# Attention beside a long convolution: U interleaved by VectorE instead of GpSimd, last taps on SP's queue, other durations in the plan

## The chip, the core and the metric

The kernel runs on one core of a Trainium2 chip. The core has TensorE (PE in the profile, its weight loads PEld), ScalarE (ACT), VectorE (DVE), GpSimd (POOL) and SyncE (SP), each with a list of instructions of its own that it takes in order, and 16 DMA engines. The metric is the device time of one execution in microseconds (us).

## What is computed

Two branches over a sequence of 2048 rows of 448 features, mixed by a gate per row:

```python
g = sigmoid((x * gate_w).sum(-1, keepdims=True))
q, k, v = (x @ wq) in 16 heads of 28, x @ wk, x @ wv          # one key and value head for all
a = concat(softmax(q k^T / sqrt(28)) v) @ wo
K = einsum("dn,dnl,dn->dl", C, exp(dt*A*l), dt*B).real          # 256 complex modes, l = 0..2047
b = causal_convolution(x, K) + x * Dskip                        # per feature; by FFT in the reference
out = g * a + (1 - g) * b
```

The reference calls the second branch with the same x: u is x, and the input B_u is not read.

## The kernel before, in words

**Attention.** For each of 4 query blocks of 512 rows and 4 groups of 4 heads (16 steps i), 64 tiles of scores (16 key tiles by 4 heads, 128 x 512 each) are made on TensorE (L1289, or L1312 with the masked copy qM of the queries), turned into exponentials on ScalarE (L1344, in turns over three and two tiles at once, 410 instructions in all, written to a ring of 15 tiles) and multiplied with the values on TensorE (L1362). Five PSUM banks hold the scores, so the matmuls of one turn fill the banks that the turn before has left. VectorE copies each step's result away (L1127) and divides it (L1139); the output projection of a block (`outp`, L1109) is folded into O on VectorE (`fold`, L1118). `qproj` (L857, L863, L866, L869) makes the next step's queries, and GpSimd's queue issues the DMAs that spread them into qM.

**Convolution.** The 448 features are taken in 14 blocks c of 32. `masters` (L896 to L916) squares the modes' factors, `tables` (L936 to L986) builds tables of powers on VectorE, five levels of products (L950) and sums (L965) of doubling size, then L973, L979 and L986. `kgen` (L1009) makes 32 features' taps from a table on TensorE in two halves; VectorE copies each to kstg (L1019), and four DMAs per half write it to a scratch tensor KP in DRAM. `tload` reads KP back as shifted rows (T or, late, U's space) on SP's queue. `conv` (L1071) multiplies the taps with U, VectorE scales the product (L1080), L1091 transposes it, and VectorE adds it to O (L1100). Each block has two convolutions, 28 in all.

**U.** U is x with its rows interleaved, so that a matmul can read it as weights. SP's queue loads it into O as 16 strips in two groups of eight (("ust", 0) and ("ust", 1), in `loads`). `prep_u` then copies it, half of the features into U and half into a part of T, with two strips to an instruction: 16 GpSimd copies (L598) of 128 x 448 bf16. Six shifted copies U<-U per group of blocks follow on SP's queue once all of the first half's are done; the other half is moved to U later by `ufill`. O is set to zero when all 16 copies are done.

**The order of the work** is not written by hand. Each operation is entered with an engine, a duration in ns, what it reads and writes, and a priority `pr` (lower first). `Prog.schedule` runs a greedy simulation: among all operations it takes the one that could start earliest, then by `pr`, and so fixes every engine's list. Durations come from `el(n, rate, fix) = fix + n / rate`, with 68 ns and 0.96 elements per ns by default. A GpSimd operation of 500 ns or more keeps VectorE from starting for 0.55 of its time. `LAZY` and `SLACK` add some ns to the time at which an operation of a given `pr` counts as ready on TensorE or VectorE. Where TensorE would be idle long enough, a filler matmul (L1271) is put in. On the chip the lists are kept as they are, with semaphores between the engines: an operation that is ready later than the simulation had it holds up all behind it on its engine.

Of the kernel before, what the change touches and what calls it, by code (L numbers as in the profile page):

```python
# [12 lines left out]
P = 128  # L13
# [29 lines left out]
GATE = (30, 35)  # L43
WARM = 64
NEWQ = 15
STORES = (401, 405, 408)
SIN2PI = 6.2831850
SQ = 1.0 / math.sqrt(DH)
# [36 lines left out]
class Prog:  # L85
# [9 lines left out]
    POOL = (7, 5)  # L95
    SLACK = {"pe": 500.0, "dve": 300.0}
    FAR = 2500.0
    LAZY = {1.2: 200.0, 1.4: 200.0, 1.55: 200.0, 1.6: 200.0}
    LATE = 1000.0
    FILL, FWIN, FLOW = 215.0, 4000.0, 0.8  # L100

# [284 lines left out]
def el(n, rate=0.96, fix=68):  # L386
    return fix + n / rate
# [14 lines left out]
class Kernel:  # L402
# [75 lines left out]
    def consts(self):  # L478
        pg = self.pg
        V = lambda b, off, n: b.v(0, P, off, [[1, n]])  # L480
        pm = lambda ap, val, ns, key, pr=0: pg.op("pool", lambda e: e.memset(ap, val), ns, wr=key, pr=pr)
        dm = lambda ap, val, ns, key, pr=0: pg.op("dve", lambda e: e.memset(ap, val), ns, wr=key, pr=pr)
        sm = self.small
        dm(V(self.cst, 512, 256), 0.0, 170, [("cst", 1)])
        pm(V(self.ident, 0, P), 1.0, 200, ["id"])
        pg.op("pool", lambda e: e.affine_select(
            out=V(self.ident, 0, P), in_=V(self.ident, 0, P), compare_op=ALU.is_equal, fill=0.0,
            base=0, pattern=[[-1, P]], channel_multiplier=1), 300, rd=["id"], wr=["id"])
        dm(self.tab.v(0, P, 4 * D, [[QS, 4], [1, 64]]), 0.0, 200, ["xpad"])
        dm(self.Wk.v(0, P, 28, [[32, 16], [1, 4]]), 0.0, 100, ["Wk"])  # L490
        dm(self.Wq.v(0, P, 28, [[32, 64], [1, 4]]), 0.0, 300, ["Wq"])
        dm(self.vaug.v(0, P, 28, [[32, 16]]), 1.0, 80, ["va"])
        dm(self.vaug.v(0, P, 29, [[32, 16], [1, 3]]), 0.0, 80, ["va"])
        dm(V(sm, 1, 1), 0.5 * math.pi, 60, ["hpi"])
        pg.op("dve", lambda e: e.tensor_reduce(V(sm, 0, 1), self.ident.v(0, P, 28, [[32, 4]]), AX.X, ALU.max),
              160, rd=["id"], wr=["s0"], pr=0.1)
        pm(V(self.Wm, 0, P), 0.0, 100, ["Wm"], 1)
        for hb in range(4):
            pm(self.Wm.v(32 * hb, 28, 32 * hb + 28, [[1, 1]]), -1.0, 100, ["Wm"], 1)
        for k in range(2):  # L500
            pm(V(self.qM, k * XQ, XQ), 0.0, 1800, [("qM", k)], 1.5)
        self.identg = self.kstg.cast(F32)
        pm(V(self.identg, 0, P), 1.0, 200, [("kst", 0)], 2)
        pg.op("pool", lambda e: e.affine_select(
            out=V(self.identg, 0, P), in_=V(self.identg, 0, P), compare_op=ALU.is_equal, fill=0.0,
            base=0, pattern=[[-1, P]], channel_multiplier=1), 300, rd=[("kst", 0)], wr=[("kst", 0)], pr=2)
        self.sel = self.onT.cast(F32)
        for k, base in enumerate((-30, -31, -32)):
            ap = self.sel.v(0, 16, 128 * k, [[32, 4], [1, 32]])
            pm(ap, 1.0, 200, [("sel", k)], 3)  # L510
            pg.op("pool", lambda e, ap=ap, base=base: e.affine_select(
                out=ap, in_=ap, compare_op=ALU.is_equal, fill=0.0, base=base,
                pattern=[[0, 4], [1, 32]], channel_multiplier=2), 300, rd=[("sel", k)], wr=[("sel", k)], pr=3)
        dm(self.one.v(0, P, 0, [[1, 2]]), 1.0, 60, ["one"], 3)
        dm(self.one.v(0, P, 2, [[1, 2]]), 0.0, 60, ["one"], 3)
# [69 lines left out]
    def prep_u(self):  # L585
        pg = self.pg
        done = []
        for half in range(2):
            for k in range(2):
                for j in range(0, 8, 2):  # L590
                    jj = 8 * k + j
                    if half == 0:
                        dst, w = self.U.v(0, P, 2 * jj, [[128, UA // 2], [1, 4]]), ["Uz", ("Ub", k)]
                    else:
                        dst, w = self.T.v(0, P, UB + 2 * jj, [[32, UA // 2], [1, 4]]), ["rawdone", ("UB", k)]
                    key = ("ustd", half, jj)
                    done.append(key)
                    pg.op("pool", lambda e, dst=dst, jj=jj, half=half: e.tensor_copy(  # L598
                        dst, self.O.v(0, P, jj * D + half * UA, [[2, UA // 2], [D, 2], [1, 2]])), 660,
                        rd=[("ust", k)] + ([] if half else []), wr=w + [key], pr=1 + half)  # L600
        for k, (c0, c1) in enumerate(((0, 2), (2, 5), (5, 9), (9, 14))):
            n = 16 * (c1 - c0)
            pg.dma(self.ushift(self.U, 1024 * c0, self.U, 1024 * c0, 128, n, 1), (6 * 16 * n, 64), f"du{k}", rd=[("Ub", 0), ("Ub", 1)],
                   wr=[("Uc", c) for c in range(c0, c1)], pr=0.35 if k < 2 else 0.9 + 0.1 * k, slow=True, iss=700.0)
        V0 = lambda b, off, n, r: b.v(0, P, off, [[n // r, r], [1, n // r]])
        Z = lambda n, r: self.cst.v(0, P, 512, [[0, r], [1, n // r]])
        pg.dma([(V0(self.O, 0, 16 * D, 32), Z(16 * D, 32))], (4096, 448), "zO", rd=[("cst", 1)] + done,
               wr=[(x, q) for q in range(16) for x in ("O", "Oz")], pr=1)
# [311 lines left out]
    def tables(self, c):  # L920
# [21 lines left out]
        for lv in range(5):  # L942
            w = 1 << lv
            m = mo + lv * 256
            n = w * EW
            so, do = lo + (32 - w) * 2, lo + (32 - 2 * w) * 2
            to, tw, kt = (lo, 16, [("lt", s, 0), ("lt", s, 1)]) if lv < 4 else (FM, 32, [("Fm", 0), ("Fm", 1)])
            kd = [lk(3 + 2 * lv), lk(4 + 2 * lv)]
            late = [lk(11), lk(12)] if lv < 4 else []
            mul = lambda e, o, a, b: e.tensor_tensor(o, a, b, ALU.mult)  # L950
            if lv == 0:
                A = lambda off, st: tab.v(0, P, off, [[st, 2], [64, 64], [1, 2]])
                M = lambda off, st: mbf.v(0, P, off, [[st, 2], [2, 64], [1, 2]])
            else:
                A = lambda off, st, w=w: tab.v(0, P, off, [[64, 128], [2, w], [1, 2]] if st == PL else [[st, 2], [64, 64], [1, 2 * w]])
                M = lambda off, st, w=w: mbf.v(0, P, off, [[2, 128], [0, w], [1, 2]])
            for k in range(2):
                src = A(so, PL) if k == 0 else A(so + PL, -PL)
                vo(lambda e, k=k, src=src, A=A, M=M, m=m, do=do, to=to, tw=tw: mul(
                    e, A(do + k * PL, to + k * tw - do - k * PL), src, M(m, 128)),  # L960
                   2 * n, done[0] + done[1][2:] + mk(lv), [kd[k], kt[k]] + late)
            for k in range(2):
                dv = tab.v(0, P, do + k * PL, [[64, 64], [1, 2 * w]])
                tv = tab.v(0, P, to + k * tw, [[64, 64], [1, 2 * w]])
                vo(lambda e, dv=dv, tv=tv, k=k: e.tensor_tensor(dv, dv, tv, ALU.add if k else ALU.subtract), n, [kt[k], kd[k]], [kd[k]])  # L965
            done = [done[0] + [kd[0]], done[1] + [kd[1]]]
        done = done[0] + done[1][2:]
        rk = [("tmp", 0), ("tmp", 1)]
# [20 lines left out]
    def kgen(self, c):  # L989
# [7 lines left out]
        for q in range(2):  # L997
            G = self.grp()
            for k in range(4):
                m = 4 * q + k  # L1000

                def mm(e, m=m, k=k, G=G):
                    for comp in range(2):
# [10 lines left out]
                                    tile_position=(0, 64 * u), skip_group_check=True)  # L1014
                    return r
                pg.op("pe", mm, 245, mode="h", ni=16, rd=keys,
                      wr=[(X, q), ("kst", q)], pr=1.4, lock=G if k == 0 else None)
            o = 512 * q
            pg.op("dve", lambda e, o=o, G=G: e.tensor_copy(ko.v(0, P, o, [[1, 512]]), G.v(0, P, 0, [[1, 512]])),  # L1019
                  el(512), rd=[(X, q)], wr=[("kst", q)], pr=2, unlock=G)  # L1020
            lst = [(dram(self.KP, (32 * c + 16 * q + 2 * (g % 2) + g // 2) * KW, [[64, 32], [4 * KW, 4], [1, 64]]),
                    ko.v(32 * g, 32, o + 64 * (g % 2), [[128, 4], [1, 64]])) for g in range(4)]
            pg.dma(lst, (512, 128), f"kw{q}", rd=[("kst", q)], wr=[("KP", c, q)], pr=0, eng="pool", extra=1800)

    def tbufs(self):
        home = [(self.T, T0 + k * TW, 0) for k in range(NTR)] + [(self.U, 0, 42), (self.U, TW, 50)]
# [76 lines left out]
    def outp(self, qc, tt):  # L1103
# [4 lines left out]
        for g in range(4):  # L1108
            pg.op("pe", lambda e, g=g: e.matmul(  # L1109
                px(), self.onT.v(0, P, g * 512 + 128 * tt, [[1, 128]]), self.Wo.v(0, P, g * D, [[1, D]]),  # L1110
                start=(g == 0), stop=(g == 3), tile_position=(0, 0), skip_group_check=True), 200,
                rd=["Wo"] + [("on", gg) for gg in range(4)], wr=[X], pr=1.2, lock=G if g == 0 else None)
        self.fold(qc, tt, px, 0, D, [X], unlock=G)

    def fold(self, qc, tt, px, off, n, rd, unlock=None):
        tl = 4 * qc + tt
        ov = self.O.v(0, P, D * tl + off, [[1, n]])
        self.pg.op("dve", lambda e: e.scalar_tensor_tensor(ov, px(), self.gt.v(0, P, tl, [[1, 1]]), ov, ALU.mult, ALU.add),  # L1118
                   el(n), rd=rd + ["gt"], comm=(("O", tl), ("Oz", tl)), pr=2, unlock=unlock)

    def norm(self, i):
        pg = self.pg
# [120 lines left out]
    def main(self):  # L1243
# [32 lines left out]
        def qk(s):  # L1276
# [63 lines left out]
            for t in ts:  # L1340
# [2 lines left out]
            n = len(ts)  # L1343
            pg.op("act", lambda e: e.activation(expT.v(0, P, 512 * es[0], spread(es, n)),  # L1344
                                                self.psS.v(0, P, 512 * bs[0], spread(bs, n)),
                                                AF.Exp, scale=SQ), 58 + 512 * n / 1.2, rd=bk, wr=ew, pr=0)

        def pv(v):
            ts = range(4 * v, 4 * v + 4)
# [104 lines left out]
```

## Time and profile before

| | us |
|---|---|
| median of 3 runs | 502.0 (500.86 to 503.79) |
| the profiled execution | 503.36 |
| its span in the profile | 501.5 |
| first exponential (L1344) starts | 19.35 |
| last exponential ends | 494.73 |
| POOL's sixteen copies (L598) | 43.36 to 56.30 |
| first convolution matmul (L1071) starts | 99.2 |
| last table step on VectorE (L986) ends | 454.08 |

Line numbers are those of the kernel before. L151 is the helper that issues all DMAs; L482 and L481 are the memsets on VectorE and on GpSimd. In the timeline, a row has the start, the length, the engine, the line, the operation, what is written and read, the shapes and how many instructions were merged; in brackets stands the time that the engine was idle ahead of it and what released it. Instructions of one engine overlap in the records by their start-up, 0.1 to 0.2 us, so the step from one start to the next is shorter than a length.

### The profile page before, as it was taken

The numbers are of one execution on the slowest core, as the hardware profiler recorded it, in microseconds if no ns is written. First come the engines' busy times: TensorE is split into PE (matmuls) and PEld (weight loads), VectorE is DVE, ScalarE is ACT, GpSimd is POOL, SyncE is SP. The second block draws the span as 40 slices with busy tenths as digits, with TensorE's granted clock in tenths as the row PEclk, the third lists the DMA queues.
The fourth block names the chain that finished last, engine by engine and source line by source line (L and its number), as shares of the span: only waits on it lengthen the run. The fifth ranks groups of instructions, "written<-read, shape, count | busy, mean of one in ns | idle before, by whom it ended". The sixth has DMA issues, their size and how long they took to land.

```text
span 501.5 us, 17468 instructions
## 1 busy us (share of the span) xinstructions
PE 468.2 (93%) x7651; PEld 213.7 (43%) x7734; DVE 455.7 (91%) x862; ACT 485.0 (97%) x435; POOL 166.5 (33%) x308
## 2 busy tenths in 40 slices
PE   8899999999999999989999999988999999999997
PEld 6532233344443334444443434434444253455563
DVE  5999999999999999999999999989999999994222
ACT  5999999999999999999999999989999999999995
POOL 5106534233243243224316124521512540535110
PEclk9799999999999999999999999989999999999999
DMA  8997289847519348995934861799692666777942
GB/s 236 324 190 191 26 189 132 274 118 241 158 25 284 102 125 208 276 242 114 272 87 104 237 180 46 225 250 263 175 255 36 195 205 182 218 204 209 298 153 78
DMA packets 151527, 91.86 MB, mean 183 GB/s; under 512 B 83514, under 2 KB 147436, under 8 KB 151452
## 3 DMA queue, kind: packets, MB, share of 16 engines
q1 hardware_dynamic: 141962, 81.05, 60.2%
q0 software_dynamic: 8960, 9.54, 7.8%
q8 instruction: 60, 0.98, 0.8%
q10 hardware_dynamic: 530, 0.17, 0.2%
q14 instruction: 15, 0.12, 0.1%
HBM read 73.61 MB, written 5.23 MB: 157 GB/s over the span
## 4 chain that ended last, share of the span: by engine, by line
DVE 57%; ACT 23%; PE 16%; DMA 2%; issue 1%; SPq 0%
ACT expT L1344 22%; DVE tab L950 19%; DVE tab L965 10%; DVE tab L979 4%; DVE tmp L973 3%; DVE msq L896 3%; PE psS L1289 2%; DVE kstg L1019 2%; PE psB L1362 2%; PE psS L1312 2%; DVE cst L1080 2%; DMA T<-KP_scratch 1%; DVE seedz L898 1%; DVE mbf L916 1%; DVE acc L1127 1%; DVE qT L869 1%
## 5 line engine op out<-in xcount | busy, mean ns | idle before, releaser
L1344 ACT ACTIVATE expT<-psS 128x1536 bf16<-128x1536 f32 (+1 forms) x410 | 466.2, 1326 | 4.6 <-PE psS L1289 2.8
L950 DVE TENSOR_TENSOR tab<-tab,mbf 128x512 bf16<-128x512 bf16 (+4 forms) x140 | 140.4, 1007 | 0.0
L1289 PE MATMUL psS<-qT,kT 29*128 29x512 bf16 x654 | 92.2, 387 | 8.1 <-ACT expT L1344 4.0
L1362 PE MATMUL psB<-expT,vaug 128*32 128x512 bf16 x960 | 96.1, 391 | 0.4 <-DVE acc L1127 0.3
L151 POOL DMA_DIRECT2D KP_scratch<-kstg x112 | 61.6, 557 | 101.5 <-DVE kstg L1019 101.0
L1312 PE MATMUL psS<-qM,kT 128*128 128x512 bf16 x234 | 76.1, 383 | 11.8 <-issue 8.1
L965 DVE TENSOR_TENSOR tab<-tab 128x256 bf16<-128x256 bf16 (+4 forms) x140 | 78.6, 585 | 0.0
L1362 PEld LDWEIGHTS psB<-expT,vaug 128*32 128x32 bf16 x960 | 24.6, 93 | 70.6 <-issue 68.8
L1271 PE MATMUL psB<-ident,one 128*128 128x512 bf16 x168 | 53.9, 383 | 0.1
L151 POOL DMA_DIRECT2D qM<-qT x64 | 32.6, 515 | 58.5 <-DVE qT L869 37.2
L1289 PEld LDWEIGHTS psS<-qT,kT 29*128 29x128 bf16 x654 | 22.6, 91 | 55.9 <-ACT expT L1344 40.8
L151 POOL DMA_DIRECT2D rdenB<-R_scratch x60 | 30.3, 510 | 48.1 <-DMA R_scratch<-denT 48.0
L1071 PE MATMUL psS<-T,U 128*26 128x128 bf16 (+3 forms) x1792 | 40.0, 223 | 0.7 <-DMA T<-KP_scratch 0.7
L1071 PEld LDWEIGHTS psS<-T,U 128*26 128x26 bf16 (+3 forms) x1792 | 31.6, 106 | 15.0 <-issue 9.6
L1071 PE MATMUL psX<-T,U 128*32 128x128 bf16 (+3 forms) x1472 | 33.8, 222 | 1.5 <-issue 1.2
L979 DVE TENSOR_TENSOR tab<-tab,tmp 128x1984 bf16<-128x1984 bf16 x28 | 32.6, 1188 | 0.1
L1071 PEld LDWEIGHTS psX<-T,U 128*32 128x32 bf16 (+3 forms) x1472 | 25.4, 106 | 14.1 <-issue 10.9
L1312 PEld LDWEIGHTS psS<-qM,kT 128*128 128x128 bf16 x306 | 18.8, 97 | 26.6 <-ACT expT L1344 17.0
L973 DVE TENSOR_TENSOR tmp<-tmp,mq 128x64 bf16<-128x64 bf16 (+4 forms) x70 | 26.1, 373 | 0.2
L1271 PEld LDWEIGHTS psB<-ident,one 128*128 128x128 bf16 x168 | 15.2, 97 | 23.0 <-issue 13.1
L896 DVE TENSOR_TENSOR msq<-seedz 128x512 f32<-128x512 f32 (+1 forms) x40 | 24.9, 622 | 0.0
L151 POOL DMA_DIRECT2D R_scratch<-denT x15 | 8.5, 565 | 48.1 <-DVE denT L1133 20.1
(186 smaller groups left out, 522.3 us busy)
## 6 DMA issues: line engine op xcount, KB each, us to landing
T<-KP_scratch SPq DMA_DIRECT2D x204, 272.0 KB, 5.0
U<-KP_scratch SPq DMA_DIRECT2D x20, 272.0 KB
rdenB<-R_scratch POOLq DMA_DIRECT2D x60, 64.0 KB
U<-cst SPq DMA_DIRECT2D x1, 3584.0 KB, 23.8
qM<-qT POOLq DMA_DIRECT2D x64, 32.0 KB, 4.6
tab<-in_A_x_dram SPq DMA_DIRECT2D x4, 448.0 KB, 6.1
O<-in_A_x_dram SPq DMA_DIRECT2D x16, 112.0 KB, 2.9
O<-cst SPq DMA_DIRECT2D x1, 1792.0 KB, 10.6
```

The source lines that it names most:

```text
L151: return [e.dma_start(o, i, **kw) for o, i in pairs]
L896: pg.op("dve", lambda e: e.tensor_tensor(m2(msq), z2, z2, ALU.mult), el(2 * n), rd=[kr, ki] + first, wr=["msq"], pr=pr)
L950: mul = lambda e, o, a, b: e.tensor_tensor(o, a, b, ALU.mult)
L965: vo(lambda e, dv=dv, tv=tv, k=k: e.tensor_tensor(dv, dv, tv, ALU.add if k else ALU.subtract), n, [kt[k], kd[k]], [kd[k]])
L973: vo(lambda e, w=w, lv=lv: e.tensor_tensor(rho.v(0, P, (32 - 2 * w) * 2, [[64, 32], [2, w], [1, 2]]), rho.v(0, P, (32 - w) * 2, [[64, 32], ...
L979: vo(lambda e, k=k: e.tensor_tensor(tab.v(0, P, FM + k * FP + 2, [[64, 32], [2, 31], [1, 2]]), tab.v(0, P, lm + k * PL + 62, [[64, 32], [- ...
L1071: r = e.matmul(ps.v(32 * j, 32 - m0, 128 * k, [[1, 128]]), self.U.v(0, P, (4 * gi + j) % UA // 2 * 128 + 2 * (2 * m0 + par) + j % 2, [[4, ...
L1271: return e.matmul(t.v(0, P, off, [[1, 512]]), self.one.v(0, P, 2, [[0, P]]), self.ident.v(0, P, 0, [[0, 4], [1, P]]), start=b != 6, stop=b ...
L1289: r = e.matmul(self.psS.v(0, P, 512 * b, [[1, 512]]), kT.v(32 * h, DH + 1, 128 * kt, [[1, 128]]), qT.v(32 * h, DH + 1, 512 * (i % 2), [[1, ...
L1312: return e.matmul(self.psS.v(0, P, 512 * b, [[1, 512]]), kT.v(0, P, 128 * kt, [[1, 128]]), self.qM.v(0, P, (i % 2) * XQ + 512 * h, [[1, 51 ...
L1344: pg.op("act", lambda e: e.activation(expT.v(0, P, 512 * es[0], spread(es, n)), self.psS.v(0, P, 512 * bs[0], spread(bs, n)), AF.Exp, scal ...
L1362: r = e.matmul(self.psB.v(32 * h, 32, 0, [[1, 512]]), vaug.v(0, P, 32 * kt, [[1, 32]]), expT.v(0, P, 512 * ring[t], [[1, 512]]), start=(kt ...
```

## The change

`prep_u` interleaves U by four VectorE copies in place of sixteen GpSimd copies. U, T and O are read as 32-bit words (two bf16 values each), and one copy takes eight strips: 128 x 896 words, inner step 224 words at the source, runs of eight words at the destination. Each is entered with 1000 ns, on "dve" instead of "pool", with the same reads, writes and priorities. The two memsets of qM go from GpSimd to VectorE, entered with 1130 ns and `pr` 0.5 (before: 1800 and 1.5). For c = 13 the KP writes go to SP's queue (700 ns an issue) instead of GpSimd's. The rest changes numbers that the plan goes by: `kgen` has `pr` 1.15 instead of 1.4, `outp` 1.58 instead of 1.2, and LAZY's entries follow, all still 200; the first-level products and sums of `tables` are entered at 1.09 and 1.16 elements per ns instead of 1.92; `fold` at 0.86 instead of 0.96; an exponential over n tiles with 46 + 428 n ns instead of 58 + 512 n / 1.2.

```diff
+LASTQ = 13
-    LAZY = {1.2: 200.0, 1.4: 200.0, 1.55: 200.0, 1.6: 200.0}
+    LAZY = {1.15: 200.0, 1.55: 200.0, 1.58: 200.0, 1.6: 200.0}
...
-            pm(V(self.qM, k * XQ, XQ), 0.0, 1800, [("qM", k)], 1.5)
+            dm(V(self.qM, k * XQ, XQ), 0.0, 1130, [("qM", k)], 0.5)
...
+        U4, T4, O4 = (b.cast(mybir.dt.int32) for b in (self.U, self.T, self.O))
         for half in range(2):
             for k in range(2):
-                for j in range(0, 8, 2):
-                    jj = 8 * k + j
-                    if half == 0:
-                        dst, w = self.U.v(0, P, 2 * jj, [[128, UA // 2], [1, 4]]), ["Uz", ("Ub", k)]
-                    else:
-                        dst, w = self.T.v(0, P, UB + 2 * jj, [[32, UA // 2], [1, 4]]), ["rawdone", ("UB", k)]
-                    key = ("ustd", half, jj)
-                    done.append(key)
-                    pg.op("pool", lambda e, dst=dst, jj=jj, half=half: e.tensor_copy(
-                        dst, self.O.v(0, P, jj * D + half * UA, [[2, UA // 2], [D, 2], [1, 2]])), 660,
-                        rd=[("ust", k)] + ([] if half else []), wr=w + [key], pr=1 + half)
+                if half == 0:
+                    dst, w = U4.v(0, P, 8 * k, [[64, UA // 2], [1, 8]]), ["Uz", ("Ub", k)]
+                else:
+                    dst, w = T4.v(0, P, UB // 2 + 8 * k, [[16, UA // 2], [1, 8]]), ["rawdone", ("UB", k)]
+                key = ("ustd", half, k)
+                done.append(key)
+                pg.op("dve", lambda e, dst=dst, k=k, half=half: e.tensor_copy(
+                    dst, O4.v(0, P, (8 * k * D + half * UA) // 2, [[1, UA // 2], [D // 2, 8]])), 1000,
+                    rd=[("ust", k)] + ([] if half else []), wr=w + [key], pr=1 + half)
...
-                   2 * n, done[0] + done[1][2:] + mk(lv), [kd[k], kt[k]] + late)
+                   2 * n, done[0] + done[1][2:] + mk(lv), [kd[k], kt[k]] + late, 1.92 if lv else 1.09)
...
-... n, [kt[k], kd[k]], [kd[k]])
+... n, [kt[k], kd[k]], [kd[k]], 1.92 if lv else 1.16)
...
-                      wr=[(X, q), ("kst", q)], pr=1.4, lock=G if k == 0 else None)
+                      wr=[(X, q), ("kst", q)], pr=1.15, lock=G if k == 0 else None)
...
-            pg.dma(lst, (512, 128), f"kw{q}", rd=[("kst", q)], wr=[("KP", c, q)], pr=0, eng="pool", extra=1800)
+            if c < LASTQ:
+                pg.dma(lst, (512, 128), f"kw{q}", rd=[("kst", q)], wr=[("KP", c, q)], pr=0, eng="pool", extra=1800)
+            else:
+                pg.dma(lst, (512, 128), f"ks{q}", rd=[("kst", q)], wr=[("KP", c, q)], pr=0, iss=700.0)
...
-                rd=["Wo"] + [("on", gg) for gg in range(4)], wr=[X], pr=1.2, lock=G if g == 0 else None)
+                rd=["Wo"] + [("on", gg) for gg in range(4)], wr=[X], pr=1.58, lock=G if g == 0 else None)
...
-                   el(n), rd=rd + ["gt"], comm=(("O", tl), ("Oz", tl)), pr=2, unlock=unlock)
+                   el(n, 0.86), rd=rd + ["gt"], comm=(("O", tl), ("Oz", tl)), pr=2, unlock=unlock)
...
-                                                AF.Exp, scale=SQ), 58 + 512 * n / 1.2, rd=bk, wr=ew, pr=0)
+                                                AF.Exp, scale=SQ), 46 + 428 * n, rd=bk, wr=ew, pr=0)
```

More of the change, by code (lines that the diff above doesn't have):

```diff
@@ L964, in tables @@
                 tv = tab.v(0, P, to + k * tw, [[64, 64], [1, 2 * w]])
-                vo(lambda e, dv=dv, tv=tv, k=k: e.tensor_tensor(dv, dv, tv, ALU.add if k else ALU.subtract), n, [kt[k], kd[k]], [kd[k]])
+                vo(lambda e, dv=dv, tv=tv, k=k: e.tensor_tensor(dv, dv, tv, ALU.add if k else ALU.subtract), n, [kt[k], kd[k]], [kd[k]], 1.92 if lv else 1.16)
             done = [done[0] + [kd[0]], done[1] + [kd[1]]]
```

## The prediction

> **What bounds the kernel now.** I read the busy shares first, then the chain of work that ended last, then ScalarE's timeline, since ScalarE turned out to be the busiest engine.
>
> ```profile
> PE 468.2 (93%) x7651; PEld 213.7 (43%) x7734; DVE 455.7 (91%) x862; ACT 485.0 (97%) x435; POOL 166.5 (33%) x308
> ...
> DVE 57%; ACT 23%; PE 16%; DMA 2%; issue 1%; SPq 0%
> ```
>
> ScalarE (ACT) is busy 97% of the span, yet the chain lies on VectorE (DVE) for 57%. Both are true: ScalarE runs its 410 exponentials (L1344) almost without a gap, and what small gaps it has come, through TensorE's queue, mostly from VectorE. GpSimd (POOL) at 33% bounds nothing. ScalarE's timeline from 31 us on (start, length, instructions merged; in brackets the idle time ahead and who ended it):
>
> ```profile
> 31.47 34.34 ACT L1344 ACTIVATE expT<-psS 128x1536 bf16<-128x1536 f32 x30
> 66.04 104.57 ACT L1344 ACTIVATE expT<-psS 128x1536 bf16<-128x1536 f32 x92 [0.23 <-PE psS L1289]
> 171.13 63.41 ACT L1344 ACTIVATE expT<-psS 128x1536 bf16<-128x1536 f32 x56 [0.53 <-PE psS L1289]
> 234.84 93.53 ACT L1344 ACTIVATE expT<-psS 128x1536 bf16<-128x1536 f32 x82 [0.29 <-PE psS L1289]
> 329.29 1.45 ACT L1344 ACTIVATE expT<-psS 128x1536 bf16<-128x1536 f32 x1 [0.92 <-PE psS L1289]
> 330.97 1.02 ACT L1344 ACTIVATE expT<-psS 128x1024 bf16<-128x1024 f32 x1 [0.23 <-PE psS L1312]
> 332.71 10.71 ACT L1344 ACTIVATE expT<-psS 128x1536 bf16<-128x1536 f32 x9 [0.72 <-PE psS L1289]
> 344.29 150.44 ACT L1344 ACTIVATE expT<-psS 128x1024 bf16<-128x1024 f32 x133 [0.87 <-PE psS L1312]
> ```
>
> The brackets show 3.8 us of waiting, but neighbours in a pipeline overlap by about 0.2 us, so shorter waits hide. The true loss is seen from the starts. Where nothing disturbs it, an exponential over three tiles and one over two form a pair:
>
> ```profile
> 79.73 1.45 ACT L1344 ACTIVATE expT<-psS 128x1536 bf16<-128x1536 f32 x1
> ...
> 90.90 1.57 ACT L1344 ACTIVATE expT<-psS 128x1536 bf16<-128x1536 f32 x1
> ```
>
> Ten instructions start from the first of these up to the second, five pairs: 11.17 / 5 = 2.235 us (steps of 1.331 and 0.904). From 31.47 to the start of the last one (494.73, where the last row ends, less its 0.73: 494.00) lie 201 pairs and one step of 1.33, which is 450.6 us undisturbed; 462.5 were used. **ScalarE loses 12.0 us** in this stream. Ahead of it stand 31.5 us of preparation, behind it 6.8 us of last projection and store. Of the 12.0, 3.4 fall in one stage, 327 to 345 us (0.92 ahead of 329.29, and from 329.29 to 344.29 15.0 us for 12.5 us of work): TensorE waits there for a load of taps (the chain has 7.05 us of "DMA T<-KP_scratch" from 320.73), its granted clock then reads 0.50 from 330.0 to 333.4, and the transfers' share is 1.0.
>
> The other 8.6 us are many small stalls of one kind:
>
> ```profile
> 169.74 0.33 PEld L1091 LDWEIGHTS psS<-ident,cst 128*64 128x64 bf16 x16 [1.02 <-DVE cst L1080]
> ...
> 170.69 0.10 PEld L1289 LDWEIGHTS psS<-qT,kT 29*128 29x128 bf16 x3
> ...
> 171.13 1.45 ACT L1344 ACTIVATE expT<-psS 128x1536 bf16<-128x1536 f32 x1 [0.53 <-PE psS L1289]
> ```
>
> TensorE takes its list in order. A matmul of the convolution (L1091) waits for VectorE's product cst, 1.02 us at its weight load, and the score matmul behind it (L1289), which needs nothing of VectorE, feeds ScalarE late. Measured as a step between starts less 0.904 or 1.331, eleven stalls of over 0.2 us have a tap-generating, output or projection matmul in front that VectorE released (105.8, 110.5, 139.9, 169.4, 233.5, 265.4, 285.9, 297.5, 308.9, 407.7, 414.6 us): 0.26 + 0.29 + 0.23 + 0.86 + 0.41 + 0.27 + 0.32 + 0.23 + 0.28 + 0.21 + 0.27 = 3.6 us. So VectorE was later than the list had assumed.
>
> **The change, part by part.**
>
> *Sixteen GpSimd copies out, four VectorE copies in.* The POOL copies (L598) run from 43.36 to 56.30 us and cost VectorE time:
>
> ```profile
> 42.13 0.29 DVE L900 TENSOR_TENSOR seedz<-msq 128x128 f32<-128x128 f32 x1
> ...
> 45.98 0.70 POOL L598 COPY T<-O 128x448 bf16<-128x448 bf16 x1
> 45.99 0.26 DVE L965 TENSOR_TENSOR tab<-tab 128x128 bf16<-128x128 bf16 x1
> 46.17 0.66 DVE L900 TENSOR_TENSOR seedz<-msq 128x128 f32<-128x128 f32 x1
> ```
>
> L900 takes 0.29 us alone and 0.66 under a copy: it ends only when the copy has. Fifteen VectorE instructions from 43.8 to 56.4 are longer in this way by 0.22 to 0.37 us than their shape is elsewhere: 4.6 us in all. The four new copies move 896 words of 32 bits each. No row is that shape. The two nearest have 896 32-bit elements: L795, one source, 0.62 us (0.54 to the next start), and L792, two operands, 1.08 us (1.0 to the next). I take 4 x 0.54 = 2.2, because the copy has one source in SBUF as L795 does; the other end is 4 x 1.0 = 4.0 (the new operands step over strides, which L795 doesn't). VectorE gains 2.4 us, at worst 0.6.
>
> [...]
>
> The interleaved U is ready some 5 us earlier than 55.7, where the shifted copies U<-U are issued now. That is worth nothing: the first convolution matmul (L1071) starts at 99.2 us. What covers it is the table work; without cover it would be 5 us.
>
> *Two memsets of qM from POOL to VectorE.* On POOL each takes 1.81 us. VectorE's f32 rows give 0.93 elements per ns (512 in 0.69 us, 256 in 0.42), so 1024 words are 1.1 us each, 2.2 in all. VectorE idles 1.87 us up to 3.55 and 1.95 up to 5.66, with loads that don't move. Cost 0; if both fell behind 5.66, 2.2 us on the way to the first score.
>
> *Last taps on SP.* The eight KP writes of c = 13 leave POOL (2.2 us for four, the first at 457.27) for SP's queue at 0.62 us each. Behind them on SP stand only the T loads that wait for them; SP issues nothing from 454.1 to 462.35. Taps come between 1 us earlier and 1 us later. The last convolution's product is at 487.6, ScalarE's end at 494.7: 7 us cover this, so 0.
>
> *Durations and slack in the plan.* This edit adds no work; it reorders every list. The old plan prices the pair at 1338 + 911 = 2249 ns, 14 above the measured 2235: 2.9 us too slow over 201 pairs. It prices the first-level products (L950, 256 elements) at 0.20 us where the step is 0.30 (307.00 to 307.30), and the sums (L965, 128) at 0.135 where it is 0.18: two each per table, 14 tables, 4.0 us too fast on VectorE; and twelve output folds by 0.05 too fast, 0.6. Against it, it charges VectorE 16 x 0.55 x 0.66 = 5.8 us for the copies that cost 4.6. So the list takes VectorE to be 6.3 us earlier against ScalarE than it is: the same size as the 8.6 us of small stalls. In the new plan the pair is 2232 and the tables and folds are right, the copies at 1.0 us too dear if anything. So I expect the eleven stalls to go, and nothing of the stalls below 0.2 us, where the list leaves no room. The bounds are 0 (each wait comes back elsewhere) and 6.3.
>
> **Sum.** Head 0, U 0 on the path (it is part of VectorE's lateness), taps 0, waits -3.6 + 0.1: -3.5 us. The profiled execution took 503.36 us (span 501.5 and 1.9 around it) and comes to 499.9. It lies 1.4 above the median of the runs shown (502.0), so the forecast is **498.5 us**.
>
> **The rivals.**
> *The tap stage goes too.* The new order moves the bursts of U<-T and T loads apart, and the 3.4 us of 327 to 345 vanish besides: 495.1. For it: the stage comes once, from a coincidence of transfers. Against: the loads are all still there. The half clock is part of its price: the trace has it from 19.4 to 26.2 us (granted clock 0.50) and here from 330.0 to 333.4. [...]
> *Nothing comes of it.* A new list has new small waits in place of the eleven; the time is what it was, 502.0 give or take 2.5. For it: there are 14 tables and 28 convolutions to wait for in any order.
> *VectorE waits for u (slower).* Place: the copies stand in VectorE's list, which is taken in order, and wait for the loads of u; on POOL this cost nothing (1.37 us idle ahead of 43.36). The old list has them behind the qM issue that follows L869's end at 39.72; if the new one has them right there, VectorE stands still up to 43.36, 3.6 us, and again for the second eight loads, issued by 45.83 and landing 2.9 later, 48.7: another 4.2. The chain is VectorE's from 55 to 308 us, so a wait W that the plan didn't expect reaches ScalarE whole: 498.5 + W, up to 506.3. It decides (slower than 504.5) from W = 6. Against it: the old plan's place is right to within 1.4 us.
> [...]
>
> **How the numbers follow.** About 0.5%, 2.5 us, is what a measurement of this kernel can tell from no change. Forecast 0.43 (its own range 496 to 499.5), tap stage 0.12, nothing 0.28, VectorE's wait or a second late tap load 0.17. Faster by over 0.5%: 0.43 + 0.12 = 0.55; same 0.28; slower 0.17. The range reaches from 495.0 (half of the tap stage's case below it) to 505.0 (half of the slower case above it): 0.06 + 0.09 left out.
>
> **What would show it.** Right: L598's four copies take 0.6 us on VectorE, L898, L900 and L916 are 0.29 there; the eleven brackets "<-DVE kstg" and "<-DVE O" ahead of L1009 and L1109 shrink; exponentials from 31 to 494 lose 8.5 us instead of 12. Wrong: idle on VectorE ahead of the copies released by "DMA O"; the loss stays at 12; memsets of qM behind 5.66; a first exponential later than 19.35; a tail longer than 6.8 us.

## The result and the profile after

After takes 505.2 us (median of 8 runs, 504.28 to 507.98), before 502.5 in the same series (8 runs, 500.86 to 503.95): a ratio of 1.0062, with an interval of 1.0043 to 1.0082. The change makes the kernel 0.6% slower. The profiled execution of after took 504.28 us, its span is 502.5.

The page of after, busy times and the chain of work that ended last:

```profile
PE 480.8 (96%) x7720; PEld 213.8 (43%) x7720; DVE 457.1 (91%) x868; ACT 483.8 (96%) x435; POOL 145.6 (29%) x282
...
ACT 80%; PE 15%; DVE 2%; DMA 2%; issue 1%; SPq 0%
```

GpSimd is 21 us lighter (166.5 to 145.6). VectorE, which gained four copies and two memsets, is only 1.4 us heavier (455.7 to 457.1). The chain no longer runs over VectorE (57% before, 2% now): ScalarE has become the late stream. What TensorE waited for between 31 and 450 us (times in us: total, number, longest), first in before, then in after:

```profile
PE psS L1312 <- issue: 7.3, 44, 0.3
...
PE psS L1009 <- DVE kstg L1019: 0.6, 3, 0.2
PE psS L1091 <- DVE cst L1080: 0.5, 1, 0.5
PE psS L1009 <- DVE qT L869: 0.4, 1, 0.4
```

```profile
PE psS L1292 <- ACT expT L1347: 4.5, 19, 0.6
PE psS L1315 <- ACT expT L1347: 1.1, 6, 0.2
PE psS L1074 <- DMA T<-KP_scratch: 0.6, 1, 0.6
```

The row with 44 waits for "issue" in before is no wait: the trace has 306 weight loads of L1312 and only 234 of its matmuls, and where a matmul's record is missing TensorE looks idle; for the same reason its busy time reads 468.2 us in before against 480.8 in after. The waits for VectorE that the prediction spoke of are gone; at TensorE's weight loads, those that VectorE ended fell from 19.5 to 9.1 us between 31 and 450. ScalarE loses 6.5 us from 31 us to its 376th exponential, where before lost 11.5, and starts this one at 449.73 instead of 455.56. Yet its last one starts at 493.42, against 494.00. **Some 5.8 us are won by 450 us, and all but 0.6 are lost again in the 44 us behind it**; then the tail behind the last exponential is 8.3 us instead of 6.75 (counted in every kernel from the last start plus the 0.73 us of before's row).

The loss has a place. Stretches of both kernels (window; its length, then busy time and number of instructions of each engine; last TensorE's granted clock, the share of the DMA engines and GB/s), before and then after:

```profile
470.00:478.00 8.00, 7.78 (x204) 4.49 (x196) 0.85 (x3) 8.00 (x8) 0.57 (x1) 1.00 1.07 349
478.00:487.00 9.00, 9.00 (x238) 6.16 (x240) 2.17 (x5) 9.00 (x9) 1.99 (x4) 1.00 0.48 148
```

```profile
470.00:478.00 8.00, 8.00 (x224) 5.20 (x216) 1.53 (x3) 8.00 (x8) 1.98 (x4) 1.00 1.05 312
478.00:487.00 9.00, 6.89 (x151) 4.17 (x150) 1.92 (x4) 6.12 (x6) 0.00 (x0) 0.81 0.93 282
```

From 478 to 487 us TensorE is busy 6.89 us instead of 9.00, its clock is 0.81 on average (0.50 from 482.9 to 486.3), ScalarE does six exponentials instead of nine, and the DMA engines are full where before's are half idle. TensorE's own timeline there in after (start, length; in brackets the idle time ahead):

```profile
478.75 0.63 PE L1181 MATMUL psS<-seedz 128*32 128x128 f32 x13
481.28 0.41 PE L1181 MATMUL psS<-seedz 128*32 128x128 f32 x3 [1.91 <-issue]
```

In the middle of one row of sixteen equal matmuls TensorE stands still for 1.91 us and waits for nothing that a semaphore shows ("issue"). The DMA queues from 478.4 to 481.3 us:

```profile
q1 hardware_dynamic: 895, 0.91, 99.5%
q0 software_dynamic: 26, 0.04, 5.9%
q8 instruction: 1, 0.02, 2.5%
```

One packet of the queue q8, 16384 bytes, came in this window among 0.95 MB of other traffic; it started at 478.53. The page counts 60 such packets, 0.98 MB, in the span; after's trace has 15,440 matmuls and weight loads of TensorE, about 60 times 256. From 200 us on, TensorE's idle times of over 0.55 us in before, after and the two shuffles below number 14. Counted through the program, 8 of them stand at the same place of a 256, within 20 instructions (one of the 8 the profile puts down to a tap load). I read a stall of this kind as TensorE at the edge of the instructions that it has, with the next packet late; the later experiments test it.

### The profile page after: what moved, and what is told of

The parts are those of the page before. It is cut to its first block, busy times and chain, and to the rows that moved or that the text cites. A ratio compares the mean times of both kernels' runs of the same rounds, so it can differ in the third digit from the quotient of the medians.

```text
span 502.5 us, 17501 instructions
## 1 busy us (share of the span) xinstructions
PE 480.8 (96%) x7720; PEld 213.8 (43%) x7720; DVE 457.1 (91%) x868; ACT 483.8 (96%) x435; POOL 145.6 (29%) x282
## 4 chain that ended last, share of the span: by engine, by line
ACT 80%; PE 15%; DVE 2%; DMA 2%; issue 1%; SPq 0%
ACT expT L1347 79%; PE psS L1315 2%; PE psS L1292 2%; DMA T<-KP_scratch 2%; PE psS L1074 1%; PE psB L1365 1%; PE psB L1274 1%; PE psB L1268 1%; PE psX L629 1%; PE psX L1074 1%; PE psS L1009 1%; PE psB L1359 1%; PE psS L1306 1%; PE psS L781 0%; PE psS L1303 0%
## 5 line engine op out<-in xcount | busy, mean ns | idle before, releaser
L1315 PE MATMUL psS<-qM,kT 128*128 128x512 bf16 x306 | 92.2, 384 | 1.5 <-ACT expT L1347 1.1
L152 POOL DMA_DIRECT2D KP_scratch<-kstg x104 | 57.3, 557 | 86.9 <-DVE kstg L1019 72.5
L965 DVE TENSOR_TENSOR tab<-tab 128x256 bf16<-128x256 bf16 (+4 forms) x140 | 77.2, 572 | 0.0
L1274 PE MATMUL psB<-ident,one 128*128 128x512 bf16 x154 | 49.3, 384 | 0.0
L1074 PE MATMUL psX<-T,U 128*26 128x128 bf16 (+3 forms) x1856 | 44.4, 223 | 1.0 <-issue 1.0
L1074 PEld LDWEIGHTS psX<-T,U 128*26 128x26 bf16 (+3 forms) x1856 | 33.4, 106 | 16.6 <-issue 11.2
L152 POOL DMA_DIRECT2D denT<-acc x15 | 10.7, 714 | 88.5 <-DVE acc L1130 88.5
L1074 PE MATMUL psS<-T,U 128*32 128x128 bf16 (+3 forms) x1408 | 32.7, 222 | 0.7 <-DMA T<-KP_scratch 0.6
L1074 PEld LDWEIGHTS psS<-T,U 128*32 128x32 bf16 (+3 forms) x1408 | 24.5, 106 | 11.2 <-issue 7.6
L1274 PEld LDWEIGHTS psB<-ident,one 128*128 128x128 bf16 x154 | 13.6, 97 | 21.4 <-issue 13.1
```

Source lines behind the costliest of these rows:

```text
L152: return [e.dma_start(o, i, **kw) for o, i in pairs]
L1074: r = e.matmul(ps.v(32 * j, 32 - m0, 128 * k, [[1, 128]]), self.U.v(0, P, (4 * gi + j) % UA // 2 * 128 + 2 * (2 * m0 + par) + j % 2, [[4, ...
L1274: return e.matmul(t.v(0, P, off, [[1, 512]]), self.one.v(0, P, 2, [[0, P]]), self.ident.v(0, P, 0, [[0, 4], [1, P]]), start=b != 6, stop=b ...
L1315: return e.matmul(self.psS.v(0, P, 512 * b, [[1, 512]]), kT.v(0, P, 128 * kt, [[1, 128]]), self.qM.v(0, P, (i % 2) * XQ + 512 * h, [[1, 51 ...
```

## The experiments

The theory at this point (A): the parts of the change cost nothing, but the new order of the lists does, by late instruction packets and by a longer tail. Its rivals: (B) the taps on SP's queue hold the last tap loads back (they were issued from 464.28 on, 462.35 in before); (C) the copies on VectorE are dear; (D) ScalarE's gain never could shorten the kernel, because VectorE's stream sets the end (its last table ends at 453.6, 454.1 in before). The ratios are to before in the same series, with 95% intervals.

**One edit at a time, the plan free to reorder.** `before_taps_sp` is before with the four lines on LASTQ, `before_u_dve` with the copies and memsets, `before_plan` with the numbers of the plan, `after_taps_pool` is after with

```diff
-LASTQ = 13
+LASTQ = 14
```

> Before with one edit: the tap writes of the last two tables' convolutions go to SP's queue, as in after. If the moved taps make the loss, by holding the T loads of the first half behind the second half's tap writes (464.28 in after against 462.35 in before), the time is 1.5 to 3 us above before. If the loss comes from the order that the new plan gives, or from VectorE's copies, it stays within 0.7 us of before (502.5).

> Before with one edit: U's four 32-bit copies and the two mask fills on VectorE instead of GpSimd. By the rows of after VectorE gives 3.7 us for the copies and no longer pays 4.6 us on fifteen neighbours, so if VectorE's stream sets the end the time is 0 to 1 us under before; if U on VectorE makes the loss, 2 to 3 us above it.

> Before with one edit: the traced durations in the plan, nothing moved. If the order that these durations give makes the loss, the time is 2 to 3 us above before, with ScalarE's stalls smaller up to 450 us and larger behind it. By my prediction's own reason, that fewer stalls of ScalarE shorten the kernel, it is 3 us under before. If VectorE's stream sets the end and the order costs nothing, it is within 0.7 us of before.

> After with its tap move taken back: the last two tables' tap writes go to GpSimd's queue again. If the moved taps make the loss, the time is that of before less up to 1 us (501.5 to 502.5); if the order makes it, it stays at 504 to 506.

Measured: taps 1.0031 (1.0006 to 1.0056), U 1.0094 (1.0069 to 1.0120), plan 1.0101 (1.0077 to 1.0125), after with taps on GpSimd 1.0068 (1.0035 to 1.0101). The first, +1.6 us, is the lower end of what its expectation gave for B. But taking the taps back doesn't help after, and in before's own order, in the next experiments, the moved taps cost nothing: B falls. U alone and the plan alone each cost as much as or more than all three together, so the parts don't add up. The run with U on VectorE also speaks against D: its last table ended at 448.1 us, 6 before that of before, and its span is 2.7 us longer. Each of these edits changes what the plan sees, and so reorders TensorE's whole list.

**Order against content.** Two shuffles change no operation:

```diff
-    SEM_NS = 56
+    SEM_NS = 55
```

(57 in the other). And in the kernels named `fixed_`, the list is made with before's operations and numbers; then only the exchanged operations are put into it, the waits are derived anew, and all else on every engine stays in before's order:

```diff
         self.order = order
+        self.replay()     # exchanges o.new for o, keeps self.seq, derives the waits
```

> Before with nothing moved and no operation changed: the planner's charge for a semaphore is 55 ns instead of 56, which only shuffles the order at near ties. If the loss of after is the price of any new order, this run is 2 to 6 us above before, with stalls of ScalarE behind 450 us as in after. If the loss comes from what the change gives the planner, it is within 1 us of before.

> The same with 57 ns instead of 56: a second shuffle of the order with nothing else changed. 2 to 6 us above before if any new order costs this, within 1 us of before if not.

> Before with every engine's instructions kept in before's order, and only U's copies exchanged: four of 32-bit words on VectorE at the place of the sixteen on GpSimd. If the copies as such cost nothing and only the new order that the planner gives is dear, the time is that of before less up to 1.5 us (4.6 us of lengthened neighbours go, 3.7 us of copies come). If the copies themselves make the 4.7 us of the run with U on VectorE alone, it is 3 to 5 us above before.

> Before in before's order, and only the last two tap writes exchanged: on SP's queue, both of them ahead of the loads that wait for them. If the move itself holds the first half's loads back, by the 1.9 us that after showed, and the end hangs on these loads, the time is 1.5 to 2 us above before; if the end has slack there, within 0.7 us of before.

> Before's order kept on every engine, with U's four copies on VectorE and the last taps on SP together: all that the change does on the chip except the new order. If the new order alone makes the loss, 500.5 to 502.5 us. If the two moves hurt one another, 504 or more.

Measured: the shuffles 1.0041 (1.0017 to 1.0065) and 1.0094 (1.0058 to 1.0129). In before's order U 0.9986 (0.9965 to 1.0007), taps 0.9982 (0.9961 to 1.0003), both 0.9966 (0.9940 to 0.9992); the two memsets of qM stay on GpSimd in these three. This settles where the loss comes from: **the change without its new order is 0.3% faster; the new order turns that into 0.6% slower, about 4.8 us (1.0062 against 0.9966 of 502 us); and an order shuffled for no reason costs 2 to 5 us too.** C falls with it. The plan foresaw none of this: it forecasts its span as 497.2 us for before, 496.3 for after, 497.2 and 497.0 for the shuffles. It does count TensorE's blocks of 256 (L92, BLOCK and FETCH): it takes a block to be there 4.8 us behind the edge ahead of it, 3.3 us for edges from 480 us on, and lets TensorE run on at that moment.

**Which stream sets the end.** In before's order, work is added to one engine, the plan not knowing of it (o.twice: the operation stands twice in the list).

> Before's order, with the two last-level products of the seventh table done twice: some 4.4 us more on VectorE near 255 us, same values. If VectorE's stream and the tail behind its last table set the end, 3.5 to 5 us above before; if ScalarE's stream sets it, 0 to 1.5 us above.

> Before's order, with the exponentials of three sets (160, 170, 180) done twice: some 4 us more on ScalarE between 180 and 210 us, same values. If ScalarE's stream sets the end, 3.5 to 5 us above before; if VectorE's stream and the tail behind it set the end, 0 to 1.5 us.

Measured: VectorE 1.0113 (1.0072 to 1.0154), ScalarE 1.0082 (1.0050 to 1.0114), that is +5.7 and +4.1 us for 4.8 us (by the ends of the sixth and seventh table) and 4.0 us (three times 1.33) of work. In both traces half clocks follow the added work, at 255.5 to 262.3 us and at 210.8 and 238.1 (mean granted clock of the execution 0.987 and 0.986, against 0.993 with U alone in the fixed order), and I count them as part of the price. Each expectation's first alternative came true, and put side by side they exclude what both supposed, that one stream sets the end: either passes its delay on in full. TensorE serves both in one fixed list, so a delay in either holds the other. D is wrong as put: VectorE's stream does not set the end alone, and neither does ScalarE's.

**Do packets wait behind DMA traffic?** In the `_late` kernels the list stays as it is, and only the three large stores of the output, which in after are issued from 476.36 us on, wait for a set of scores near 490 us:

```diff
+            if qc < 3:
+                o.hold = self.end      # scores of set 407
```

> After's own order, with the three large stores of the output held until the third set of scores from the end, so that they leave the DMA engines free from 476 to about 490 us. If TensorE's late instruction packets (478.53, 485.17 in after) wait behind these stores, the stall of 1.9 us at 479.4 and the half clock behind it go, and the time is 2 to 4 us under after. If the packets wait behind the tap loads, which stay, the stall stays and the time is within 1 us of after (505.2).

> The order of the shuffle with 57 ns, its three large output stores held in the same way. That run stalled 1.61 us at 479.27, with the half clock from 481.9, and 1.38 us at 309.0, with the half clock from 311.2. The stores can have to do with the first alone: if they have, that stall shrinks to under 0.5 us and the time falls by 2 to 3.5 us (from 1.0094 of before); the stall at 309 stays.

> The order of the run with the traced durations alone, its three large output stores held until the third set of scores from the end. That run stalled 1.27 us at 480.85 and 1.07 us at 486.85 at edges of 256 instructions. If the packets of these edges waited behind the stores, both stalls shrink to under 0.5 us and the time falls by 2 to 3 us against the run without this edit (506.7, 1.0101 of before); if not, it stays at 505.5 to 507.

> Before's order, with three more stores of 0.43 MB each behind the first large output store (some 3.5 us of all DMA engines near 475 us, into a scratch tensor that nobody reads). If TensorE's instruction packets wait behind such traffic, the packet that came at 476.08 or the one at 481.12 in before comes 1.5 to 3 us later, TensorE stalls at the edge of its 256 instructions by 1 to 3 us, and the time is 2 to 5 us above before. If the DMA engines' load near the end doesn't matter to TensorE, within 0.7 us of before.

> Before's order with U's copies on VectorE, the last taps on SP and the three large output stores held. The run without the held stores still stalled 0.7 us at 475.8; if that goes, 500.3 to 501.3 us, some 0.4 to 0.5% under before. If the held stores crowd the end (they leave from 490 us), 502 or more.

Measured: after with held stores 0.9998 (0.9971 to 1.0026, after 1.0062), the shuffle 1.0042 (1.0012 to 1.0072, was 1.0094), the plan alone 1.0037 (1.0017 to 1.0058, was 1.0101): each 2.6 to 3.2 us less for stores that leave later. After with held stores, the same window and the same matmuls as above (its lines are shifted by 45):

```profile
478.00:487.00 9.00, 8.30 (x230) 5.45 (x231) 2.34 (x5) 8.69 (x8) 0.00 (x0) 1.00 0.52 151
```

```profile
480.35 0.41 PE L1226 MATMUL psS<-seedz 128*32 128x128 f32 x3 [0.49 <-issue]
```

The DMA share falls from 0.93 to 0.52, the stall from 1.91 to 0.49 us, the clock stays at 1.00, and the last exponential starts at 490.62 instead of 493.42. In the shuffle, first as it was and then with held stores:

```profile
480.88 0.26 PE L1091 MATMUL psS<-ident,cst 128*64 128x64 bf16 x4 [1.65 <-issue]
```

```profile
480.02 0.26 PE L1136 MATMUL psS<-ident,cst 128*64 128x64 bf16 x4 [0.52 <-issue]
```

In the plan alone the expectation came true for the median and for the second stall, at 486.85, which went. The first, in the one execution that was profiled (505.4 us, against 504.4 without the edit), is longer than the 1.27 us that it was:

```profile
482.87 0.64 PE L1405 MATMUL psB<-expT,vaug 128*32 128x256 bf16 x10 [1.82 <-issue]
```

Its packet came at 480.30. The last tap loads were issued at 476.16 and took 7 us to land, and the DMA engines were full throughout from 474 to 481 us without any store, so the stores are not the only traffic that makes a packet late. The reverse experiment, 1.3 MB of stores added to before's order, gave 1.0026 (1.0005 to 1.0047): the right sign, at the lower end of what theory A gave or under it. Its stall is there, without a half clock behind it:

```profile
484.17 0.63 PE L1226 MATMUL psS<-seedz 128*32 128x128 f32 x11 [1.07 <-issue]
```

Two more kernels of the first round show the same: U alone stalls 1.82 us at 475.29 and after with taps on GpSimd 1.89 us at 485.74, both at an edge, with the half clock from 477.7 and from 487.5.

The packets themselves, from the traces. "Edge" is when TensorE entered its block of 256, "packet" the start of the packet for the next block, "goes on" when that block began:

| kernel | edge | packet (behind the edge) | goes on (behind the packet) | idle |
|---|---|---|---|---|
| before | 473.48 | 476.08 (2.60) | 478.58 (2.50) | 0 |
| after | 474.38 | 478.53 (4.15) | 481.28 (2.75) | 1.91 |
| after, stores held | 474.86 | 477.58 (2.72) | 480.35 (2.77) | 0.49 |
| shuffle 57 | 474.31 | 478.25 (3.94) | 480.88 (2.63) | 1.65 |
| shuffle 57, stores held | 474.82 | 477.77 (2.95) | 480.02 (2.25) | 0.52 |
| plan alone | 475.57 | 479.49 (3.92) | 482.13 (2.64) | 1.27 |
| plan alone, stores held | 475.76 | 480.30 (4.54) | 482.87 (2.57) | 1.82 |
| fixed order, both parts | 470.66 | 474.30 (3.64) | 476.50 (2.20) | 0.71 |
| before's order, stores added | 477.87 | 481.62 (3.75) | 484.17 (2.55) | 1.07 |

Where TensorE waits, it goes on 2.2 to 2.8 us behind the start of the packet. Elsewhere in after, at the edges crossed at 464.13 and 487.58, up to whose packets the DMA engines are busy 0.22 and 0.00 of the time, the packet starts 0.5 and 1.1 us behind the edge; here it starts 2.6 to 4.5 us behind. The 18 traces together say the same of the edges behind 440 us: where the DMA engines are busy under 0.3 in the first us behind the edge (55 edges), the packet starts 0.7 us behind it in the median and 1.7 at most; where over 0.9 (81 edges), 2.9 us in the median and 1.0 to 4.6. A block lasts some 4.3 to 6 us in this stretch, so I estimate from these figures that a packet over about 2 to 3.5 us late costs time here. Where TensorE waits in the table, the next block came 5.2 to 7.1 us behind the edge, and the plan had allowed 4.8. Whether a list made with a larger figure would be faster was not tried.

Putting the held stores into the kernel that is best so far gained nothing: 0.9999 (0.9980 to 1.0018), where 0.4 to 0.5% under before was expected; 502 or more was expected if the held stores crowd the end, and 502.5 came, but its tail of 6.75 us shows no crowding. Its stall of 0.6 us is still there (its packet comes among tap loads), and this profiled execution also lost a half clock at 330.5 us that has nothing to do with the stores. No version tried is better than before's order with the two moved parts, 0.9966.

**The longer tail.** The orders differ in where the last convolution stands. In before, 28 score matmuls and all of the output projections stand behind its last product; in after 8, in the plan alone none. Behind the last score matmul stand 39 matmuls in before, 65 in after, 121 in the plan alone. The measured tails behind the last exponential follow: 6.7 to 6.9 us in the twelve kernels with before's order, a shuffle of it or the moved taps alone (39 in each), 8.3 in the four with after's order or U alone (65), 9.5 in the two with the plan alone (121). TensorE near the end, in before and then in after:

```profile
490.63 0.35 PE L1205 MATMUL psS<-Wo,onT 128*128 128x448 bf16 x1
...
497.92 0.55 PE L1205 MATMUL psS<-Wo,onT 128*128 128x448 bf16 x2 [0.25 <-DVE onT L1184]
```

```profile
490.82 0.81 PE L1074 MATMUL psS<-U 128*28 128x128 bf16 x44
...
494.75 0.54 PE L1208 MATMUL psX<-Wo,onT 128*128 128x448 bf16 x2
...
498.76 0.92 PE L1208 MATMUL psX<-Wo,onT 128*128 128x448 bf16 x4
```

Before projects (Wo) from 490.63 on, beside its last exponentials. After still convolves at 490.82 and projects everything behind the last exponential.

So of the 4.8 us of the new order, about 3.2 go when the stores are held (1.0062 to 0.9998), in the traces by a shorter stall at the edge and no half clock behind it, and 1.6 are tail (8.3 less 6.7). The medians add up, though each comparison is uncertain by 1 to 2 us, and holding the stores in before's order won nothing, so this split is an estimate. What the medians don't show is a gain; the 2 us that the new order saves ScalarE up to 450 us against the fixed order (a loss of 6.5 instead of 8.6) are spent in the same stretch. Why the planner puts the last convolution later was not tried.

## Why the prediction was wrong

The forecast was 498.5 us, within 495.0 to 505.0; the change took 505.2.

- **The sum's only term, -3.5 us from the plan's durations, is the step that failed.** Its mechanism came true as written: VectorE's waits ahead of the score matmuls went, and ScalarE was 5.8 us ahead at 450 us. But the step priced a new list by the waits that it was made to remove and put the rest at nothing. The plan alone is 1.0101, +5.1 us, where -3.5 was forecast. In its place the runs showed late instruction packets at the edges of blocks (a stall of 1.91 us with a half clock behind it) and a tail longer by 1.6 us. The prediction held the plan's prices for ScalarE and VectorE against the trace, but not its price for a block, 4.8 us, nor where the last convolution would stand.
- **The bounds of that step, 0 to 6.3 us of gain, had no lower side.** The prediction said of "nothing comes of it" that new waits come in place of the eleven; it didn't ask what the largest new wait could be, though before's trace had one: TensorE's idle time of 1.21 us at 342.20 stands at an edge of 256.
- **ScalarE's stream as the measure, VectorE's lateness reaching it through TensorE's list:** both held. 4.0 us more on ScalarE cost 4.1, 4.8 us more on VectorE cost 5.7. Shortening ScalarE's losses up to 450 us was real, but not enough, for the end was set behind that.
- **The tap stage**, 3.4 us, went in after, as the first rival had it, but it is not the order's doing: in six profiled executions in before's order with nothing added up to 450 us, ScalarE lost 11.5, 10.6, 10.0, 9.0, 8.7 and 8.6 us up to its 376th exponential; only the first two had the half clock at 330. The profiled execution of before was a dear one, and some 1.5 to 3 of its 11.5 us were chance. Nor was all of the stage a tap load: the 0.87 us ahead of 344.29, about 1.0 of the 3.4 by the starts, stands behind TensorE's idle time at 342.20, the edge named above.
- **U's copies**: L598 takes 0.93 to 0.95 us on VectorE and 0.84 to 0.87 to the next start, where the prediction took 0.54 to the next start, the step of L795's contiguous rows:

```profile
L598 DVE COPY U<-O x2: 934/944/954, 43.2 to 46.4; 128x896 int32<-128x896 int32 x2
L598 DVE COPY T<-O x2: 936/942/947, 44.1 to 47.2; 128x896 int32<-128x896 int32 x2
```

  (ns: least, median, most.) The four take 3.8 us by their rows and 3.4 by the starts, inside the bound of 4.0, and the lengthened neighbours are back at 0.28 to 0.30. VectorE stood idle ahead of none of them, so the slower rival, VectorE waiting for u, did not come. In time 0.9986: about 0, as forecast.
- **Memsets**: 0.91 us each, at 1.6 and 2.8 us, hidden; the first exponential at 18.72 (19.35). Right.
- **Taps on SP**: 0.9982 in a fixed order. Right in time, though "between 1 us earlier and 1 us later" missed the first half's loads: they stand behind the second half's writes and were 1.9 us later.

The case "slower" had 0.17, and it rested on VectorE's wait for u and on a second late tap load. The places that decided, late instruction packets and the tail, were not among the rivals.

## What to carry to other kernels

An edit to a planner's numbers is not an edit without cost: the new list is a new draw, and here two draws for no reason cost 2 and 5 us. Test the moved work in the old order, and the new order without the moved work, before either is credited; and where a stall has "issue" as its releaser in the middle of equal matmuls, count instructions to the edge of a block (of 256 here) and look at what the DMA engines carry just then. Where the plan has a figure for that too, hold it against the trace like the others.

## What the runs showed of the hardware

- In after, 60 packets of 16384 bytes came on the queue q8 for 15,440 matmuls and weight loads of TensorE, about one per 256. In the 18 traces, behind 440 us, such a packet starts 0.7 us behind the edge in the median where the DMA engines are busy under 0.3 in the first us, and 2.9 where over 0.9, up to 4.6.
- Stalls at an edge of 1.65 us and more near 480 us (after, shuffle 57, the plan with held stores, U alone, after with taps on GpSimd) each came with a granted clock of 0.50 for 3.4 us that began within 2 us of the stall's end (at 482.86 in after, the stall's end at 481.28). Of the others, 1.04 us at 469.2 (shuffle 55) and 1.38 at 309.0 (shuffle 57) did so too, and 1.04 at 458.1 (after), 1.27 and 1.07 (the plan alone) and 1.69 at 310.6 (shuffle 57 with held stores, at the place of the 1.38) did not. The same idle time of 1.04 us thus came with a half clock in one trace and without one in another; what decides it is not shown.
- A strided copy of 896 32-bit words from SBUF to SBUF took 0.94 us on VectorE in after (L598), against 0.62 for 896 contiguous ones with one source in before (L795).
